# Another order for the 2986 operations of an attention and hardswish FFN kernel

## The chip, the cores and the metric

The kernel runs on one core of a Trainium2 chip. The metric is the device time of one execution in microseconds (us), as the median of several runs. The engines are TensorE (PE, matmuls), VectorE (DVE), ScalarE (ACT), GpSimd (POOL) and SyncE (SP). Each executes its own instructions one after the other; SP and POOL also issue transfers (DMA).

## The reference

```python
def _attn_ref(x, state):                     # x [8, 8, 512, 64], state [8, 8, 32, 64]
    scores = scale * np.matmul(x, state.transpose(0, 1, 3, 2))
    a = softmax(scores);  xread = np.matmul(a, state)
    scores2 = scale * np.matmul(state, x.transpose(0, 1, 3, 2))
    a2 = softmax(scores2);  sread = np.matmul(a2, x)
    return np.concatenate([xread, sread], axis=2)

def _moe_ref(x, w_in, w_out):                # x: 4352 rows of 512, w_in [512, 2048], w_out [2048, 512]
    h = x @ w_in
    g = h * np.clip(h + 3.0, 0.0, 6.0) / 6.0
    return g @ w_out
```

The softmax over the last axis is written out in the reference (the maximum is subtracted, and the sum divided out). The attention's result, with the heads side by side, is the input of the second function. All data are float32.

## The kernel before

The work is staged by batch. For each of the eight batches the kernel computes the scores of its 512 tokens against its 32 states per head, both softmaxes, the product of the state with the first weight (so that tokens pass straight to the hidden layer, `wp`), and then sixteen steps over the hidden layer, each of 128 of the 2048 hidden columns; a last sixteen steps treat the state rows of all batches. The steps of one batch run on TensorE while the other engines prepare the next batch.

A step has these parts. `first` (or `first_grouped`) multiplies the attention weights `aT` by `wp` into a bank `ps_h` on TensorE. The gate follows: ScalarE (L1250, L1413 or L1677) and VectorE (L1252, L1416 or L1680, with additions at L1261 for grouped steps) make `g` or `G`. It is split in a high part `g_hi` (ScalarE, L467, L472 or L494) and a low part `g_lo`. The low part is made on VectorE (L468 or L473), or, in the "far" form, VectorE negates the high part (L495) and POOL adds the value with an accumulating transfer (L497). `second` multiplies both parts by the second weight into the accumulators `acc`. All matmul products go through one helper, L1178.

To prepare a batch, SP loads x in the layout for scores as sixteen transfers of 64 KB into `raw` (L686, eight per half) and again for the reads as `xb` (L668, four of 256 KB); VectorE transposes each half (`tmp<-raw`, L846), TensorE makes the scores of both halves (`both<-tmp,stT`, L700) and, in the same group, what the states read of the batch before (`ps_h<-xb,raw`, L1134). The turned weights for that read are made by a VectorE transposition (L1096) and sixteen moves of 32 KB on SP (`raw<-raw`, L1103). In the first 100 us the weights arrive too, in a packed form that ScalarE and VectorE decode (L571, L576), and `w_out` is split in a high and a low part (L605; later POOL adds the parts by transfers at L1654 so that a 16-bit form can be used).

What sets the order: the kernel first collects all operations in a list (`Plan.add`), with their engine, what they read and write and their buffers. A table of numbers, `ORDER`, then says in which order they are issued. `Plan.order` walks that table, asserts that every operation comes behind those it depends on, and gives each buffer user a place; `Plan.issue` emits the instructions in this order, for all five engines. So every engine, and SP's and POOL's queues of transfers among them, executes its part of the table in the table's order, and an operation that has to wait holds up those behind it on its engine.

Of the kernel before, what the change touches and what calls it, by code (L numbers as in the profile page):

```python
# [68 lines left out]
1 0 5 2 3 4 24 79 92 27 34 11 29 31 6 35 30 36 28 37 32 43 38 33 44 39 45 49 40 46 47 41 50 56 48 42 51 52 61 57 25 53  # L69
58 80 62 54 26 59 55 63 74 81 64 130 75 65 82 77 60 93 14 78 68 66 76 19 67 87 69 94 71 88 95 107 70 72 89 108 96 114  # L70
90 73 97 109 12 91 429 110 7 102 13 154 111 132 115 161 103 113 112 85 104 127 105 8 116 106 120 83 117 121 171 9 84
126 118 131 122 144 133 119 15 129 134 86 137 16 128 138 10 135 145 136 123 17 152 124 166 100 125 153 169 18 151 167
98 170 194 168 146 99 188 101 157 147 20 183 211 148 21 196 215 186 149 150 201 155 187 217 210 184 158 22 216 164 23
195 189 156 178 223 185 213 159 165 193 206 139 225 190 174 214 160 141 218 426 208 191 224 219 212 162 222 204 142
163 228 220 140 192 202 430 175 209 238 229 431 271 172 221 247 236 143 205 173 235 239 203 237 230 234 176 240 259
179 177 244 260 233 181 261 254 243 182 231 207 245 180 262 427 246 263 264 505 232 290 338 241 272 281 322 274 273
291 242 286 250 275 295 251 248 276 292 282 288 249 279 287 277 283 252 297 278 280 289 284 253 299 255 506 285 256
296 293 337 308 257 300 258 317 305 265 294 332 267 301 309 266 298 335 268 306 336 269 315 428 307 333 310 302 304
334 323 314 270 318 339 303 311 319 775 320 324 364 507 352 358 325 341 226 316 359 340 313 353 321 355 368 360 354
342 361 403 312 504 326 365 369 362 327 363 343 198 404 373 412 366 367 370 344 399 405 371 375 345 508 417 372 346  # L80
347 348 374 422 401 349 424 376 418 423 400 328 419 402 420 350 408 421 425 394 406 329 351 411 395 410 330 396 409
413 407 495 397 414 509 331 432 398 415 496 416 439 511 377 447 464 441 227 440 448 468 497 437 382 514 438 385 433
465 393 513 462 199 469 386 498 457 356 434 466 389 499 435 388 463 458 387 471 510 459 467 460 481 436 516 470 461
380 517 478 357 392 479 515 444 477 390 472 487 378 482 473 476 445 512 489 379 525 474 535 629 475 391 483 519 384
488 381 502 518 197 486 383 500 484 443 501 536 442 485 503 631 446 520 537 541 200 630 452 572 449 538 450 634 539
456 590 632 543 454 550 575 451 521 542 577 453 522 579 540 455 480 573 523 551 558 580 635 552 574 530 569 633 578
570 636 576 571 640 591 544 638 524 592 545 637 546 644 563 493 606 547 494 526 549 607 593 564 548 568 531 565 589
650 608 594 492 595 581 491 566 609 596 586 642 587 612 661 582 639 567 613 588 583 626 643 666 597 614 641 669 623
667 532 776 618 610 777 584 677 628 670 527 585 490 662 624 528 668 778 529 620 685 779 621 553 684 663 625 682 780
664 619 700 678 615 665 598 627 679 683 617 533 680 708 599 534 616 701 709 622 690 600 611 702 695 707 681 703 706  # L90
784 645 805 704 710 717 655 715 601 554 656 740 782 711 555 657 559 602 705 560 716 741 781 785 714 561 658 562 742
748 747 743 659 603 746 712 660 796 713 604 556 744 557 605 745 754 797 771 803 798 807 773 799 783 812 772 651 800
765 646 806 804 801 652 787 766 653 802 654 794 767 725 691 770 671 724 692 793 718 672 696 817 720 697 721 788 698
723 792 673 768 789 719 795 674 769 722 827 693 774 818 694 824 790 819 699 825 647 791 820 826 675 828 823 676 834
829 749 832 930 833 836 730 835 830 837 731 863 838 786 839 857 726 831 728 759 877 727 858 821 732 648 822 859 733
887 884 760 860 729 882 761 865 750 861 883 900 862 751 762 869 885 910 878 763 864 912 764 755 879 906 870 931 841
756 867 868 866 880 907 889 917 901 881 902 929 909 757 918 911 758 888 813 908 919 846 913 922 814 886 649 920 923
925 1012 903 921 808 752 753 809 927 1006 1013 904 928 905 1017 1014 1008 1015 1009 734 1005 1010 847 1016 962 815 848
851 816 1019 999 914 1018 895 915 963 1020 890 969 916 1004 1000 964 926 842 924 810 735 1007 965 1041 1001 852 1002
966 1011 853 843 967 932 849 736 854 844 1003 737 855 975 856 1067 689 935 891 1069 970 850 1071 892 968 933 936 1070  # L100
845 1042 1047 896 971 934 1054 973 946 1065 897 1049 1051 1037 1043 974 1023 972 937 1059 1028 1044 1022 947 1039 1038
1052 1027 1053 1068 1021 1060 1045 1048 1040 1046 1050 686 1086 938 1025 1076 811 1061 1026 1057 939 688 1084 1024
1082 1062 1058 840 1064 1055 1066 1094 1063 949 1056 1088 1077 1103 940 1099 1072 1078 1083 1104 1101 941 898 1106
1079 942 1105 1087 1095 1100 1107 1080 1074 1073 1081 1102 1115 948 1075 1085 1089 1113 1119 950 1096 1090 1117 943
1202 1097 1121 893 1203 1098 894 1092 1091 1116 1127 1118 1114 1130 1108 1093 1133 1126 944 1120 1128 1109 1129 1132
1205 1204 1134 1110 1206 1122 1111 738 1161 1112 1123 1142 899 945 1162 1140 1146 1124 739 1131 1164 1144 1125 1148
1163 1165 1135 1141 1145 956 1255 1149 1136 1155 957 1137 1160 1150 1153 1256 1166 951 958 1258 1257 1151 1147 1259
1154 1167 1158 1138 1143 1156 1182 959 1152 1168 1189 960 1183 1157 1169 961 1191 1184 1196 1159 1139 871 1291 1185
872 1193 1294 1170 1176 1292 1194 1186 1190 1195 976 1171 1207 1187 1172 1034 993 1192 1173 1035 1239 1188 1208 1032
1036 1209 1179 1178 1240 687 1180 1210 1199 1033 1175 1241 1177 1181 1030 1211 1174 1200 1260 1296 1212 1218 988 1198  # L110
1213 1250 1251 1293 1197 1214 991 1249 1242 1261 1253 1029 1247 994 1248 987 1243 1254 1252 1221 1262 1031 1244 1215
995 1276 992 996 1245 978 1263 1246 1289 1295 981 1217 1277 1264 1219 985 1222 1216 1278 1265 977 1269 1220 1283 982
1285 1266 983 1287 1279 1267 1319 1280 989 873 979 997 874 1273 986 1297 1335 998 984 1320 990 1290 1288 1327 980 1281
1321 1286 1284 1201 1367 1282 1224 1322 1329 1275 1336 1345 1331 1237 1333 1368 1337 1318 875 1383 1369 876 1370 1298
1338 1323 1227 1339 1324 1238 1371 1230 1328 1381 1312 1228 1347 1332 1271 1225 1274 1377 1325 1233 1343 1313 1301
1326 1349 1315 1334 1330 1226 1268 1375 1314 1229 1300 1344 1302 1379 1231 1346 1340 1223 1303 1342 1272 1232 1270
1341 1236 1304 1390 1234 1348 1396 1299 1394 1384 953 1305 1407 1372 955 1385 1395 1382 1235 1373 1408 1380 1376 1386
1374 1393 1378 1316 1409 1397 1391 1392 1387 1398 1423 1410 1388 1513 1442 1400 1389 1399 1419 1411 1424 1435 1317
1402 1434 1432 1412 1576 1425 1401 1431 1413 1577 1420 1439 1414 1422 1426 1417 1440 1350 1416 1443 1421 1433 1579
1415 1427 1362 1437 1444 1418 1428 1452 1363 1441 1436 1306 1438 1360 1445 1454 1429 1471 954 1446 1430 1462 1359 1403  # L120
1447 1357 1405 1473 1361 1463 1580 1485 1356 1307 1456 1477 1578 1353 1464 1358 1448 1450 952 1465 1451 1449 1475 1308
1365 1508 1352 1469 1514 1509 1351 1491 1457 1487 1478 1355 1453 1466 1455 1511 1489 1366 1479 1493 1467 1364 1512
1354 1480 1470 1472 1510 1494 1490 1474 1481 1476 1613 1468 1482 1504 1500 1495 1616 1492 1548 1483 1614 1503 1496
1486 1484 1501 1617 1505 1544 1615 1506 1488 1546 1497 1515 1309 1498 1404 1310 1499 1406 1559 1535 1545 1311 1551
1564 1502 1550 1563 1529 1536 1461 1530 1516 1531 1517 1566 1565 1518 1547 1549 1537 1507 1560 1552 1532 1538 1519
1567 1666 1553 1581 1539 1669 1540 1570 1554 1562 1561 1582 1670 1597 1541 1583 1555 1568 1635 1556 1542 1557 1584
# [1794 lines left out]
```

## Time and profile before

| what | value |
|---|---|
| median of 3 runs (lowest to highest) | 604.08 us (602.52 to 604.81) |
| the profiled execution | 604.03 us |
| its span, first to last instruction | 602.2 us |
| granted TensorE clock, mean | 0.998 |
| busy: PE, DVE, ACT, POOL | 98%, 80%, 65%, 15% |

The busy share of an engine is the time in which it executed something, over the span. Two engines can each be busy and wait for one another at some places, so the shares alone do not show what a change of order is worth; the rows below go by stretch and by wait. The names in a row are those of the program: `out<-in`, with L and a number for the line.

### The profile page before, as it was taken

Reading aid. Unit: us, or ns where it says so; the run is one execution under the profiler, and the core shown is the slowest. Engines: PE = TensorE matmul, PEld = TensorE weight load, DVE = VectorE, ACT = ScalarE, POOL = GpSimd, SP = SyncE. Lnnn points to the kernel's source line nnn. Section 1 sums busy time; section 2 is a strip of 40 time slices with the busy share of each in tenths; the row PEclk is TensorE's granted clock in tenths of the full one; section 3 lists DMA queues with packets and bytes.
Section 4 is the critical chain, followed back from the end, with each engine's and each line's share of the span. In section 5 each row is a group of like instructions: output and inputs, shape, how many; then the busy total and the mean of one; then the engine's idle time right before and its main releaser. Section 6 shows DMA issues by size and latency. Waiting matters only on the chain. (4 is left out here: it accounts for less than half of the span.)

```text
span 602.2 us, 13365 instructions
## 1 busy us (share of the span) xinstructions
PE 590.8 (98%) x5331; PEld 453.2 (75%) x5331; DVE 480.4 (80%) x911; ACT 389.3 (65%) x637; POOL 90.3 (15%) x112
## 2 busy tenths in 40 slices
PE   8999999999999999998999999999999999999997
PEld 7577678768654445886778887888888878888875
DVE  5988996579767998887998988977898977876332
ACT  5888868867868876746465746566555655563432
POOL 2000000103444312211101111212111201111000
PEclk9999999999999999999999999999999999999999
DMA  8999124647898955896625684578534642323001
GB/s 284 355 214 318 62 84 123 130 106 137 118 125 107 125 136 63 125 169 113 114 67 62 138 131 86 69 143 121 102 48 83 123 80 33 66 32 67 2 30 42
DMA packets 101951, 68.24 MB, mean 113 GB/s; under 512 B 67712, under 2 KB 94976, under 8 KB 101504
## 3 DMA queue, kind: packets, MB, share of 16 engines
q0 software_dynamic: 14400, 21.37, 28.7%
q1 hardware_dynamic: 87200, 45.82, 28.2%
q8 instruction: 42, 0.69, 0.5%
q10 hardware_dynamic: 288, 0.20, 0.1%
q14 instruction: 21, 0.17, 0.1%
HBM read 33.41 MB, written 8.91 MB: 70 GB/s over the span
## 5 line engine op out<-in xcount | busy, mean ns | idle before, releaser
L1178 PE MATMUL ps_h<-aT,wp 128*128 128x256 f16 (+2 forms) x1146 | 164.1, 292 | 0.0
L1178 PEld LDWEIGHTS <-g_hi 128*128 128x128 f16 x1344 | 129.8, 98 | 36.8 <-issue 5.1
L1178 PE MATMUL acc<-w,g_hi 128*128 128x256 f16 (+1 forms) x704 | 129.0, 297 | 0.0
L1178 PEld LDWEIGHTS <-wp 128*128 128x128 f16 x1056 | 103.0, 98 | 23.8 <-issue 1.1
L1178 PE MATMUL acc<-T,g_hi 128*128 128x256 f16 x640 | 100.5, 273 | 0.0
L1178 PE MATMUL acc<-w,g_lo 128*128 128x256 f16 (+1 forms) x352 | 82.2, 297 | 2.6 <-DVE g_lo L468 2.6
L1178 PEld LDWEIGHTS <-g_lo 128*128 128x128 f16 x672 | 65.1, 98 | 21.5 <-DVE g_lo L468 2.9
L1250 ACT ACTIVATE G<-ps_h,three 128x512 f32<-128x512 f32 x55 | 42.7, 777 | 34.5 <-PE ps_h L1178 19.6
L1178 PE MATMUL acc<-T,g_lo 128*128 128x256 f16 x320 | 62.7, 273 | 0.3 <-DMA g_lo<-g 0.2
L497 POOL DMA_DIRECT2D g_lo<-G x35 | 30.1, 861 | 176.3 <-DVE g_lo L495 95.7
L1261 DVE TENSOR_TENSOR G<-G 128x256 f32<-128x256 f32 (+1 forms) x110 | 52.8, 484 | 1.4
L1178 PE MATMUL acc<-w_out_hi,g_hi 128*128 128x512 f32 x124 | 49.8, 402 | 0.0
L1178 PE MATMUL acc<-w_out_hi,g_lo 128*128 128x512 f32 x124 | 48.3, 390 | 0.0
L1178 PE MATMUL acc<-w_out_lo,g_hi 128*128 128x512 f32 x124 | 48.3, 390 | 0.0
L494 ACT CAST g_hi<-G 128x896 f16<-128x896 f32 x35 | 32.7, 935 | 19.9 <-DVE G L1261 16.9
L1252 DVE SCALAR_TENSOR_TENSOR G<-G,ps_h 128x512 f32<-128x512 f32 x55 | 37.5, 682 | 8.1 <-ACT G L1250 7.9
L1413 ACT ACTIVATE g<-ps_h,three 128x512 f32<-128x512 f32 x48 | 34.1, 715 | 11.3 <-PE ps_h L1178 8.8
L497 POOL DMA_DIRECT2D g_lo<-g x25 | 22.2, 888 | 109.7 <-DVE g_lo L495 64.5
L1416 DVE SCALAR_TENSOR_TENSOR g<-g,ps_h 128x512 f32<-128x512 f32 x48 | 32.6, 682 | 6.8 <-ACT g L1413 6.7
L1654 POOL DMA_DIRECT2D w_out_hi<-w_out_lo x16 | 16.4, 1253 | 113.1 <-ACT g_hi L472 92.4
L468 DVE SCALAR_TENSOR_TENSOR g_lo<-G,g_hi 128x896 f16<-128x896 f32 (+1 forms) x30 | 25.8, 863 | 8.8 <-ACT g_hi L467 5.0
L467 ACT ACTIVATE wp<-both 128x512 f16<-128x512 f32 x40 | 22.7, 595 | 14.7 <-PE both L700 14.7
(200 smaller groups left out, 981.8 us busy)
## 6 DMA issues: line engine op xcount, KB each, us to landing
xb<-in_x_dram SPq DMA_DIRECT2D x32, 256.0 KB, 3.4
g_lo<-G POOLq DMA_DIRECT2D x35, 224.0 KB, 4.1
raw<-in_x_dram SPq DMA_DIRECT2D x112, 64.0 KB, 3.3
out_dram<-ot SPq DMA_DIRECT2D x10, 512.0 KB, 3.2
early<-in_moe_w_in_dram SPq DMA_DIRECT2D x5, 1023.0 KB, 6.3
w_out_hi<-w_out_lo POOLq DMA_DIRECT2D x16, 256.0 KB, 4.8
g_lo<-g POOLq DMA_DIRECT2D x17, 224.0 KB, 3.8
raw<-raw SPq DMA_DIRECT2D x112, 32.0 KB, 2.8
```

Of the source, the lines that this page charges most:

```text
L467: S(cost, rank, lambda: nc.scalar.mul(hi(), src(), by()), [*reads, *keys], first_, after)
L468: V_(cost, rank, lambda: nc.vector.scalar_tensor_tensor(lo(), src(), by(), hi() if hi().dtype == F16 else hi().bitcast(F32), op0=ALU.mult, ...
L494: S(cost, rank, lambda: nc.scalar.copy(hi(), src()), reads, [writes[0]], after)
L497: P__(0.87, rank, lambda: nc.gpsimd.dma_start(lo(), src(), accum_op=ALU.add), reads, [writes[1]], (), size)
L1178: nc.tensor.matmul(ps, l, r, start=start and k == 0, stop=stop and k == len(pairs) - 1)
L1250: S_(0.73, rank, lambda: nc.scalar.activation(g(), h(), AF.Relu, bias=three_of(G_SCALE / 4), scale=scales["gate7"]()), [ps, ("scale", "gat ...
L1252: V(0.63, rank, lambda: nc.vector.scalar_tensor_tensor(g(), g(), 6.0 * G_SCALE / 4, h(), op0=ALU.min, op1=ALU.mult), [ps], [key])
L1261: V(cost, rank, lambda out=out, one=one, other=other, op=op: nc.vector.tensor_tensor(blocks(*out), blocks(*one), blocks(*other), op=op), [ ...
L1413: S_(cost + (0.12 if scaled else 0.05), rank, lambda: nc.scalar.activation(g(), bank(ps)[:, :width], AF.Relu, bias=three_of(by), scale=sca ...
L1416: V(cost, rank, lambda: nc.vector.scalar_tensor_tensor(g(), g(), 6.0 * by, bank(ps)[:, :width], op0=ALU.min, op1=ALU.mult), [ps], [g_key])
L1654: X("P", 0.87, rank, lambda w=w: nc.gpsimd.dma_start(w("hi"), w("lo"), accum_op=ALU.add), [lo_key], [hi_key], after, 1.35)
```

## The change

The table `ORDER` is replaced by another permutation of the same operations. No other line differs, and the operations, their sizes and their engines are the same. A line of the table, as the diff shows it (120 such lines in all):

```diff
 ORDER = """
-1 0 5 2 3 4 24 79 92 27 34 11 29 31 6 35 30 36 28 37 32 43 38 33 44 39 45 49 40 46 47 41 50 56 48 42 51 52 61 57 25 53
...
+1 0 5 2 3 4 24 79 92 426 27 34 28 6 30 36 37 11 31 35 29 38 32 43 44 33 39 45 49 40 46 47 41 50 56 25 48 51 42 26 52
...
```

First place: VectorE while the steps of batch 3 run, at about 273 to 283 us of the profile. `G` and `g` are gates, `g_lo` a low part, `tmp<-raw` the transposition of one half of x. Before:

```order
L1252 SCALAR_TENSOR_TENSOR G<-G,ps_h 128x512
L1261 TENSOR_TENSOR G<-G 128x3x128
L1261 TENSOR_TENSOR G<-G 128x256
L846 STREAM_TRANSPOSE tmp<-raw 128x1024
L468 SCALAR_TENSOR_TENSOR g_lo<-G,g_hi 128x896
L1261 TENSOR_TENSOR G<-G 128x3x128
```

and in the changed kernel, the rows that end with the same L468:

```order
L1261 TENSOR_TENSOR G<-G 128x256
L1049 RECIPROCAL r_3003<-r_3003 128x2
L1261 TENSOR_TENSOR G<-G 128x3x128
L1096 STREAM_TRANSPOSE raw<-tmp 128x8x4x32
L885 RECIPROCAL s_3020<-s_3020 128x32
L468 SCALAR_TENSOR_TENSOR g_lo<-G,g_hi 128x896
```

and the rows around that L846, eight rows further on:

```order
L468 SCALAR_TENSOR_TENSOR wp<-both,wp 128x512
L1261 TENSOR_TENSOR G<-G 128x3x128
L495 TENSOR_SCALAR g_lo<-g_hi 128x896
L886 TENSOR_TENSOR tmp<-tmp,s_3020 128x1024
L645 STREAM_TRANSPOSE stT<-st_raw 128x128
L495 TENSOR_SCALAR g_lo<-g_hi 128x896
L846 STREAM_TRANSPOSE tmp<-raw 128x1024
L468 SCALAR_TENSOR_TENSOR wp<-both,wp 128x512
```

The transposition stood directly ahead of the split, and now stands fourteen rows behind it.

Second place: SP's queue at about 108 to 125 us, where the loads of x for batch 2 end. Before:

```order
L1103 DMA raw<-raw 32x256 x4
L668 DMA xb<-in_x_dram 128x2x256
L1103 DMA raw<-raw 32x256
L686 DMA raw<-in_x_dram 32x16x32 x3
L668 DMA xb<-in_x_dram 128x2x256
L686 DMA raw<-in_x_dram 32x16x32 x8
L668 DMA xb<-in_x_dram 128x2x256
L634 DMA st_raw<-in_state_dram 32x4x32 x4
```

and now:

```order
L686 DMA raw<-in_x_dram 32x16x32
L1103 DMA raw<-raw 32x256 x4
L686 DMA raw<-in_x_dram 32x16x32
L1103 DMA raw<-raw 32x256 x3
L686 DMA raw<-in_x_dram 32x16x32 x10
L668 DMA xb<-in_x_dram 128x2x256 x2
L634 DMA st_raw<-in_state_dram 32x4x32 x4
```

The `xb` load that stood among the last eleven loads of x now stands behind all of them.

Third place: VectorE at about 58 to 64 us, where weights are still decoded (`w_in<-wide`) beside the first batch's steps. Before:

```order
L473 TENSOR_TENSOR wp<-both,wp 128x256
L473 TENSOR_TENSOR g_lo<-g,g_hi 128x512
L576 SCALAR_TENSOR_TENSOR w_in_672<-wide,tops 128x4x128
L846 STREAM_TRANSPOSE tmp<-raw 128x1024
L576 SCALAR_TENSOR_TENSOR w_in_672<-wide,tops 128x4x128
L473 TENSOR_TENSOR g_lo<-g,g_hi 128x512
```

and now:

```order
L576 SCALAR_TENSOR_TENSOR w_in_683<-wide,tops 128x4x128 x2
L473 TENSOR_TENSOR g_lo<-g,g_hi 128x512
L846 STREAM_TRANSPOSE tmp<-raw 128x1024
L576 SCALAR_TENSOR_TENSOR early_654<-early_654,tops 128x512 x2
L473 TENSOR_TENSOR wp<-both,wp 128x512 x2
L1416 SCALAR_TENSOR_TENSOR g<-g,ps_h 128x512 x2
```

The transposition stood between the two decodes, and now stands behind both, with what follows pushed behind it.

## Rows read from the trace of the kernel before

**Rows 1.** The page, busy time: us (share of the span) xinstructions.

```profile
PE 590.8 (98%) x5331; PEld 453.2 (75%) x5331; DVE 480.4 (80%) x911; ACT 389.3 (65%) x637; POOL 90.3 (15%) x112
```

**Rows 2.** By stretch: length, busy PE, PEld, DVE, ACT, POOL, clock, DMA share, GB/s.

```profile
48.00:75.00 27.00, 26.46 (x209) 19.13 (x209) 24.56 (x39) 22.65 (x43) 0.00 (x0) 1.00 0.58 192
...
126.00:270.00 144.00, 144.00 (x1088) 91.12 (x1078) 121.26 (x234) 105.09 (x165) 43.82 (x50) 1.00 0.78 123
...
380.00:597.00 217.00, 217.00 (x2185) 184.03 (x2184) 161.87 (x316) 117.42 (x175) 24.93 (x29) 1.00 0.39 68
```

**Rows 3.** What TensorE waited for: us in total, times, longest us.

```profile
PE acc L1178 <- DVE g_lo L468: 2.6, 1, 2.6
PE both L700 <- DVE room L1584: 1.0, 1, 1.0
```

**Rows 4.** Timeline, TensorE: start us, us, operation [idle before <-releaser].

```profile
277.25 1.04 PE L1178 MATMUL acc<-T,g_hi 128*128 128x256 f16 x8
280.94 0.28 PE L1178 MATMUL acc<-w,g_lo 128*128 128x256 f16 x1 [2.65 <-DVE g_lo L468]
```

**Rows 5.** Timeline, VectorE, at the same place.

```profile
278.66 1.25 DVE L846 STREAM_TRANSPOSE tmp<-raw 128x1024 f32<-128x1024 f32 x1 [3.49 <-DMA raw<-in_x_dram]
279.83 1.05 DVE L468 SCALAR_TENSOR_TENSOR g_lo<-G,g_hi 128x896 f16<-128x896 f32 x1
```

**Rows 6.** Timeline, TensorE, score matmuls of batch 1, then of batch 2.

```profile
68.17 1.09 PE L700 MATMUL both<-tmp,stT 64*32 64x512 f32 x16
...
122.36 1.06 PE L700 MATMUL both<-tmp,stT 64*32 64x512 f32 x8
...
125.46 1.10 PE L1134 MATMUL ps_h<-xb,raw 128*32 128x64 f32 x64
```

**Rows 7.** Timeline, VectorE, ahead of the score matmuls of batch 2.

```profile
123.17 1.25 DVE L846 STREAM_TRANSPOSE tmp<-raw 128x1024 f32<-128x1024 f32 x1 [2.11 <-DMA raw<-in_x_dram]
```

**Rows 8.** Timelines of SP and POOL, then loads issued in 111.5:117.7 and 117.7:119.5.

```profile
113.83 5.34 SPq L686 DMA_DIRECT2D raw<-in_x_dram  x8
...
117.88 1.76 POOL L1654 DMA_DIRECT2D w_out_hi<-w_out_lo  x2 [10.33 <-PE acc L1178]
...
raw<-in_x_dram SPq DMA_DIRECT2D x9, 64.0 KB, 2.7
...
w_out_hi<-w_out_lo POOLq DMA_DIRECT2D x2, 256.0 KB, 4.3
raw<-in_x_dram SPq DMA_DIRECT2D x3, 64.0 KB, 3.2
```

**Rows 9.** Timeline, TensorE, 61 to 63 us.

```profile
61.49 0.39 PE L1178 MATMUL acc<-w_out_hi,g_hi 128*128 128x512 f32 x1
...
61.94 0.39 PE L1178 MATMUL acc<-w_out_hi,g_lo 128*128 128x512 f32 x1
62.82 1.09 PE L700 MATMUL both<-w_in,stT 64*32 64x512 f32 x16 [0.49 <-DVE w_in L576]
```

**Rows 10.** Timeline, TensorE, at 296 us; the transfer issued in 291:292.

```profile
296.11 0.27 PE L1178 MATMUL acc<-T,g_lo 128*128 128x256 f16 x1
296.61 0.72 PE L1178 MATMUL acc<-T,g_lo 128*128 128x256 f16 x5 [0.23 <-DMA g_lo<-g]
...
g_lo<-g POOLq DMA_DIRECT2D x1, 224.0 KB, 5.5
```

**Rows 11.** The chain that ended last, its first piece: start us, us, what.

```profile
363.84 4.92 DMA g_lo<-G
```

**Rows 12.** Timeline, SP: a load of batch 4, and the loads of batch 5.

```profile
249.70 0.63 SPq L686 DMA_DIRECT2D raw<-in_x_dram  x1
...
267.48 10.20 SPq L686 DMA_DIRECT2D raw<-in_x_dram  x13
```

**Rows 13.** The page, DMA issues: KB each, median us from issue to landing.

```profile
raw<-in_x_dram SPq DMA_DIRECT2D x112, 64.0 KB, 3.3
...
raw<-raw SPq DMA_DIRECT2D x112, 32.0 KB, 2.8
```

## What I expect, before the changed kernel has run

> **What bounds the kernel now.** The first view is the table of engines: TensorE is busy 98% of the span, VectorE 80%, ScalarE 65% [rows 1]. The second is the table by stretch: TensorE has no idle time at all from 126 to 270 us and from 380 to 597 [rows 2]. Both orders give TensorE the same matmuls, so its work is the same in both, and only its waits can change. The third view lists what TensorE waited for: one wait of 2.6 us for a VectorE split (L468), and one of 1.0 us put down to VectorE's `room` (L1584) [rows 3]; all others are below 1 us. The busy time of a matmul that stands still can hide more, so I took the timelines and compared the distance between starts with that of the same work elsewhere. That gives five places.
>
> *Place A, 278 us.* A group of eight matmuls starts at 277.25 and is busy for 1.04 us; the next starts at 280.94, after 2.65 us of waiting for L468 [rows 4]. On VectorE that split (279.83) stands directly behind a transposition of x, `tmp<-raw` at L846, which started at 278.66 after an idle time of 3.49 us that ended with a load of `raw` [rows 5]. VectorE works in order: the split had nothing to do with these loads and stood behind them.
>
> *Place B, 122 us.* Sixteen score matmuls `both<-tmp,stT` are busy for 1.09 us in batch 1; in batch 2 it takes from 122.36 to 125.46, 3.10 us, until the next kind starts [rows 6]. The excess is 3.10 - 1.09 = 2.0 us, of which the list of waits names 1.0 and the rest counts as busy. VectorE's L846, which makes their `tmp`, started at 123.17 and took 1.25 us, after 2.11 us of idle time that ended with a load of `raw` [rows 7]; I take L846, not `room`, for the releaser. Its eight loads were issued one behind the other, 5.34 / 8 = 0.67 us each, from 113.83 on. Those issued in 111.5:117.7 took a median 2.7 us to land, those in 117.7:119.5 3.2 us, with two 256 KB additions of POOL in flight, 4.3 us each, issued at 117.88 and behind [rows 8].
>
> *Place C, 62 us.* Matmuls at 62.82 waited for L576, which stood on VectorE behind another L846. Two starts at 61.49 and 61.94 set the pace, 0.23 us a matmul, so the excess is 62.82 - 61.94 - 0.23 = 0.65 us [rows 9].
>
> *Places D and E, 296 and 368 us.* The eight matmuls of rows 4 follow one another after about (1.04 - 0.28) / 7 = 0.11 us; at 296.11 one takes 0.50 us to the next, and the wait is for the transfer into `g_lo`, which took 5.5 us [rows 10]: 0.39 us. The chain of waits begins with such a transfer, 4.92 us [rows 11]; I take 0.2 us for it, half of D's.
>
> The start and the last 5 us (an eviction and a store) have the same rows in nearly the same order, so I put them at 0, with 0.4 us to either side.
>
> **The change part by part.** Nothing is added or removed; the sum is made against the profiled execution, 604.03 us, whose span is 602.2 us and which lies 0.05 us below the median of the runs, 604.08.
>
> Place A: the L846 now stands fourteen of VectorE's rows behind the split, some 10 us of TensorE's work later than before. The split would have started at 278.66 - 3.49 = 275.17 and ended 1.05 us later, before the matmuls at 277.25 began. Gain 2.65 us, if nothing new is late. What is late next: the loads of that L846. One move of the state weights (`raw<-raw`) now stands ahead of the last of them on SP, and it waits for VectorE's L1096. In the order the last load stands 6.9 us of TensorE's work ahead of L846, hardly other than the 7.2 of before; but before, SP issued late: the eight loads for the second half of batch 4 stood between its moves, the last at 249.70, and the queue was still busy with the loads for this L846 in the row from 267.48 on [rows 12]. In the new order those eight stand some 20 us of TensorE's work sooner, so SP comes to the loads of A about eight issues, 8 x 0.67 = 5 us, earlier. Landing took a median 3.3 us [rows 13]; 6.9 - 3.3 leaves some 3 us, so I take the whole 2.65, with 0 as the lower end.
>
> Place B: the eight last loads stand one SP issue sooner, 0.67 us, since the load of `xb` that was among the last eleven is now behind them. One group of three matmuls more (3 x 0.23 = 0.68 us) stands ahead of the score matmuls. So 1.35 us of the 2.0 are gone at the least; if the last load, issued about 0.65 us before 119.17, where its row ends, with 256 KB less ahead of it lands in 2.7 us and not in some 4.6 (118.52 to 123.17), all are. I take 1.5, and 0 to 2.0 as ends: POOL's additions may now be issued earlier as well. By the rows the last loads landed later when POOL's additions were in flight. The Trainium skill (DMA: Bandwidth & Descriptors, Queues, rings and completion order) says that each DMA engine goes round the queues for which it has work, packet by packet, so that a load beside an addition gets its turns only in alternation, however early it stands in its own queue. By that rule the gain would stay at the 1.35 us of the two shifts; by the landing of the undisturbed loads it would be 2.0.
>
> Place C: one L846 now stands behind the decode of the weight, and one group of matmuls more ahead of its use, so nothing of the 0.65 should be left. But VectorE is nearly full there (48:75: 24.56 of 27.00 us [rows 2]), and what it is spared at 60 us it has to do by 68 us, where a split, L846, two decodes, two evictions (L473) and two gates (L1416) now stand in one row, and the last four free the banks that the next matmuls need. I take 0 for C, with -1.25 (an L846 that TensorE waits for) and +0.65 as ends.
>
> Places D and E: between POOL's issue and the first matmul that uses the product stood 4.81 and 4.91 us of TensorE's work; now 6.34 and 5.91 (the matmuls between the two in each order, at the trace's durations). The transfers took 5.5 and 4.92 us, so both are covered: 0.6 us gained. The smallest such distance is about as before (3.27 against 3.24 us), and the median 6.56 against 6.50, so I expect no other one late by much.
>
> Everything else: at five score or product groups the VectorE operation that frees their bank now stands directly ahead of them in the order, and which of them go wrong the trace of before can't tell. The small waits of before, C, D and E, come to 0.65 + 0.6 = 1.25 us. I allow 1.2 us for new ones of that kind, with 0 and 3.9 as ends; the upper end has one more wait like A's.
>
> Sum: 2.65 + 1.5 + 0 + 0.6 - 1.2 = 3.55 us. 604.03 - 3.55 = 600.5 us.
>
> **The rivals.** First, *the waits move* and little time is gained. For it speaks that before is itself an order in which nearly all waits are hidden, and that every L846, decode or split that goes later stands ahead of something else on an engine that is 80% busy. It is one or two new waits of A's size: 604.03 - 2.65 - 1.35 - 0.6 + 2.65 = 602.1, or with two 604.7. Against it speaks that the loads and transfers at A, D and E have 1 to 3 us of cover in the new order.
>
> Second, slower: *SP's line is late where batches meet.* The place is SP's queue at 165, 295 and 370 us. The distance, in TensorE's work, from SP's last issue to the operation that needs it falls from 5.4 to 3.4 us for the first half of x of batch 3, from 5.4 to 2.95 for the moves of the state weights of batch 4 (now mixed with the x loads of batch 5), and from 11.7 to 4.7 for those of batch 5. Loads land in 3.3 us and moves in 2.8 us [rows 13], so it decides once SP stands one to three issues (0.67 us each) behind its place; from 267.48 on SP's loads came one behind the other for 10.20 us [rows 12], so it can be behind. What such a wait costs is A's 2.65 us. Three of them make 7.95: 604.03 - 4.75 + 7.95 = 607.2, and with the 1.2 us allowed above 608.4. Against it speaks that SP is through with the loads of batch 4 sooner.
>
> Third, all works and nothing new is late: 604.03 - 2.65 - 2.0 - 0.65 - 0.6 = 598.1. That the table's rows change nothing is excluded by the order of VectorE and SP at A and B.
>
> **How the numbers follow.** A measurement of this kernel can tell about 0.5% from no change, which is 3.0 us: faster is below 601.1, slower above 607.1. The forecast, with what is close to it down to 598.1, has 0.52; the waits move, 601.1 to 607.1, 0.32; SP late, above 607.1, 0.16. For the range the lower end is the case in which all works, less half a microsecond for the start, 597.7. The upper end is 606: it takes in the moved waits up to the two of A's size and 1.3 us more, and leaves out the late SP line.
>
> **What would show it.** Right: no idle time of VectorE ahead of L846 from 275 to 290 us, and no L468 among TensorE's waits there; the score matmuls near 121 us with at most 0.8 us of excess; no wait for `g_lo` by transfer above 0.2 us. Wrong: idle time of VectorE ended by `raw` loads near 165 or 290 us, or TensorE's `both<-tmp,stT` waiting for moves near 298 and 372 us (the second rival); L473 or L1416 in TensorE's waits between 55 and 80 us (the first).

## The result and the profile after

The changed kernel takes 598.5 us (598.21 to 599.02); the kernel before took 603.54 us beside it. The ratio is 0.9916 with a 95% interval of 0.9894 to 0.9938, so it is faster by 3.7 to 6.4 us. The profiled execution of after took 598.21 us with a span of 596.4 us; before's had 604.03 and 602.2 [rows 1, 2]. The pair of profiles thus differs by 5.8 us, somewhat more than the medians, which are 5.0 us apart.

The page of after, busy time; then the table by stretch (length, busy PE, PEld, DVE, ACT, POOL, clock, DMA share, GB/s):

```profile
PE 589.0 (99%) x5331; PEld 452.9 (76%) x5331; DVE 481.6 (81%) x911; ACT 389.3 (65%) x637; POOL 89.8 (15%) x112
...
48.00:75.00 27.00, 27.00 (x213) 19.99 (x213) 25.18 (x38) 22.20 (x40) 0.00 (x0) 1.00 0.53 168
115.00:126.00 11.00, 11.00 (x121) 8.31 (x120) 10.23 (x32) 7.99 (x19) 1.75 (x2) 1.00 0.63 124
...
270.00:283.00 13.00, 13.00 (x138) 11.04 (x136) 12.41 (x26) 8.87 (x13) 2.24 (x3) 1.00 0.69 106
```

The engines' work is the same; TensorE has no idle time left in the stretches of C, B and A. What TensorE waited for in after (us in total, times, longest):

```profile
PE ps_h L1890 <- PEq L1905: 0.8, 1, 0.8
PE acc L1178 <- ACT g_hi L494: 0.7, 1, 0.7
PE acc L700 <- DVE wp L473: 0.7, 1, 0.7
```

Both waits of [rows 3] are gone. The first and third row lie in the first 25 us, and the second, at 405 us, is new. At A, VectorE's timeline of after:

```profile
274.18 1.03 DVE L468 SCALAR_TENSOR_TENSOR g_lo<-G,g_hi 128x896 f16<-128x896 f32 x1
...
282.09 1.24 DVE L846 STREAM_TRANSPOSE tmp<-raw 128x1024 f32<-128x1024 f32 x1
```

Against [rows 5], the split is through 5.7 us sooner, and L846 has no idle time ahead of it. At B, the timelines of TensorE, VectorE, SP and POOL and the loads issued in 110:116.3:

```profile
121.64 1.09 PE L700 MATMUL both<-tmp,stT 64*32 64x512 f32 x16
122.66 1.10 PE L1134 MATMUL ps_h<-xb,raw 128*32 128x64 f32 x64
...
119.39 1.22 DVE L846 STREAM_TRANSPOSE tmp<-raw 128x1024 f32<-128x1024 f32 x1
...
109.96 6.82 SPq L686 DMA_DIRECT2D raw<-in_x_dram  x10
...
116.47 1.75 POOL L1654 DMA_DIRECT2D w_out_hi<-w_out_lo  x2 [12.38 <-PE acc L1178]
...
raw<-in_x_dram SPq DMA_DIRECT2D x10, 64.0 KB, 2.6
```

Against [rows 6 to 8], the score matmuls take 1.02 us to the next kind instead of 3.10, L846 ends about 1 us ahead of them, and the issue of the last of the ten loads starts at 116.14, 0.33 us ahead of POOL's additions.

Where the 5.8 us went, from the start of each matmul less the work ahead of it in its order, in the two profiles: the first 30 us 0.5, C (50 to 65 us of work) 0.9, B 2.1, A 2.9, D 0.4, E 0.3, the new wait at 405 us -0.8, and small waits elsewhere -0.5.

### The profile page after: what moved, and what is told of

Its sections match the earlier page's. It is cut to its first block, busy times and chain, and to the rows that moved or that the text cites. A ratio compares the mean times of both kernels' runs of the same rounds, so it can differ in the third digit from the quotient of the medians.

```text
span 596.4 us, 13389 instructions
## 1 busy us (share of the span) xinstructions
PE 589.0 (99%) x5331; PEld 452.9 (76%) x5331; DVE 481.6 (81%) x911; ACT 389.3 (65%) x637; POOL 89.8 (15%) x112
## 4 chain that ended last, share of the span: by engine, by line
PE 93%; DVE 2%; SPq 2%; issue 1%; ACT 1%; DMA 0%; DVEq 0%
PE acc L1178 54%; PE ps_h L1178 30%; PE both L700 5%; PE ps_h L1134 1%; SPq L1103 1%; PE acc L1449 1%; PE ps_h L1890 1%; PE ps_h L700 1%; DMA st_raw<-in_state_dram 0%; SPq L634 0%; PE both L921 0%; SPq L686 0%; DVE w_in L576 0%; ACT g_hi L494 0%; DVE ot L936 0%
## 5 line engine op out<-in xcount | busy, mean ns | idle before, releaser
L1178 PE MATMUL acc<-w,g_hi 128*128 128x256 f16 (+1 forms) x704 | 130.8, 297 | 0.0
L1178 PE MATMUL acc<-w,g_lo 128*128 128x256 f16 (+1 forms) x352 | 84.0, 297 | 0.0
L1178 PE MATMUL acc<-T,g_lo 128*128 128x256 f16 x320 | 64.2, 273 | 0.0
L468 DVE SCALAR_TENSOR_TENSOR g_lo<-G,g_hi 128x896 f16<-128x896 f32 (+1 forms) x31 | 26.3, 851 | 10.9 <-ACT g_hi L467 6.3
L467 ACT ACTIVATE g_hi<-G 128x896 f16<-128x896 f32 (+1 forms) x31 | 23.4, 758 | 17.5 <-DVE G L1261 7.4
```

The lines of the kernel that those rows point to most:

```text
L467: S(cost, rank, lambda: nc.scalar.mul(hi(), src(), by()), [*reads, *keys], first_, after)
L468: V_(cost, rank, lambda: nc.vector.scalar_tensor_tensor(lo(), src(), by(), hi() if hi().dtype == F16 else hi().bitcast(F32), op0=ALU.mult, ...
L1178: nc.tensor.matmul(ps, l, r, start=start and k == 0, stop=stop and k == len(pairs) - 1)
```

## The experiments

Each kernel is one of the two with a few numbers of `ORDER` moved. In the diffs, 1513 is the L846 of A, 1389 the split L468 behind it, 337 and 258 the L846 and the decode of C, 200 the load of `xb` and 455 the last load of x at B, 592 the score matmuls of B, 549 a group of three matmuls, and 1490 and 1893 the first matmuls with `g_lo` at D and E.

Since one profile has its chances, the same stretches were read in all runs: from the first group of `both<-w_in` at 28 us to the start of the L1134 group of batch 1 (C), from there to that of batch 2 (B), and from that of batch 4 to that of batch 5 (A and D). "As before" says that the order in the stretch is before's.

| stretch | as before | with the place changed |
|---|---|---|
| start of the first group | 27.6 to 28.8 (nine runs) | |
| C | 40.5 to 40.9 (five runs), 42.1 (one) | c_decode 41.0, five_places 40.9, c_loads 41.2, c_front 39.9; after 39.8 |
| B | 56.3 to 57.0 (six runs) | b_xb 55.4, b_additions 54.3, b_group 56.6 and five_places 55.4 (both with 0.7 more work) |
| A and D | 39.1 to 39.8 (three runs), 40.3 to 40.9 (four) | a_swap 38.2, a_back 37.0, five_places 36.4 |

What parts the two groups at A is TensorE's clock. In c_decode, b_xb, b_additions and c_loads it fell to 0.50 of full speed, 1.2 instead of 2.4 GHz, within a microsecond of the end of A's wait, and these are the four above 40 us; in before, b_group and c_front it stayed at 1.00. The waits ahead of it were of one size, 2.1 to 2.6 us in the four and 2.2 to 2.65 in the three. The stretch of b_additions at 279 to 282 us (the wait ends at 278.21), and that of before at 281 to 284 (280.94), in the columns of the table by stretch:

```profile
279.00:282.00 3.00, 3.00 (x33) 1.52 (x18) 3.00 (x7) 2.92 (x7) 0.86 (x1) 0.50 0.03 6
...
281.00:284.00 3.00, 3.00 (x44) 1.99 (x45) 3.00 (x8) 3.00 (x6) 0.46 (x1) 1.00 0.18 37
```

So A's wait costs about 1.1 us more where the clock falls behind it, and the prediction has no term for that. Why it fell in some executions and not in others stays open. The executions without a trace have a mean clock on record. It is 0.996 or 0.997 in the profiles with the fall and 0.998 to 1.000 in all others; by that mark, 0.997 or less, which is a reading and not a trace, the clock fell in 40 of the 65 executions of before that were measured beside these experiments (median 604.8 us; the other 25 have 603.2), in 6 of 10 of c_decode and 5 of 10 of c_front, where A's wait is left, in 2 of 10 of after_hold, where a wait of 1.8 us stands, and in none of the 25 of a_swap, a_back and five_places.

**a_swap: L846 one row later.**

```diff
-... 1410 1388 1513 1442 1400 1389 1399 ...
+... 1410 1388 1442 1400 1389 1513 1399 ...
```

> The order of before with one operation moved by one row of VectorE: the transposition of x (L846) of place A stands behind the split L468 instead of ahead of it. Theory 1 (the wait at A is the split's place behind a transposition whose loads are late): TensorE's wait for L468 at 278 us is gone, 2.65 us. VectorE still stands until the loads land at 278.5, some 2.3 us, with the next gates behind it; they have about 1 us of slack, so 1 to 1.5 us come back as a new wait just behind, and the time is 602.3 to 602.9 us. Theory 2 (VectorE's delay counts whatever stands behind it, the waits move): all 2.65 us come back at the next product, 603.5 to 604.1. If the row alone counted and the delay not at all: 601.4.

Measured 601.8 us against 604.52 for before, ratio 0.9961 (0.9943 to 0.9978). VectorE's and TensorE's timelines:

```profile
276.34 1.09 DVE L468 SCALAR_TENSOR_TENSOR g_lo<-G,g_hi 128x896 f16<-128x896 f32 x1 [0.78 <-ACT g_hi L467]
278.81 1.25 DVE L846 STREAM_TRANSPOSE tmp<-raw 128x1024 f32<-128x1024 f32 x1 [1.37 <-DMA raw<-in_x_dram]
...
281.89 0.27 PE L1178 MATMUL acc<-T,g_lo 128*128 128x256 f16 x1 [1.24 <-ACT ot L1287]
```

The wait for the split is gone, and VectorE still stands for the load, 1.37 us, since the split itself had to wait for ScalarE. Of the 2.65 us, 1.24 come back 3 us later, as theory 1 says, by way of ScalarE: the stretch of A and D is 1.5 us shorter than in before's profile. The time fell by more, 2.7 us, and came out 0.5 us better than theory 1's range; that fits the clock, which by the mean fell in none of its ten executions and in over half of before's.

**a_back: L846 ten rows later.**

```diff
-... 1410 1388 1513 1442 ...
+... 1414 1422 1426 1513 1417 1440 ...
```

> The order of before with the same transposition moved ten of VectorE's rows back, behind an L1261 at about 283 us, when its loads have landed. Theory 1: VectorE no longer stands idle there, A's 2.65 to 2.8 us are gone and nothing comes back: 601.2 to 601.5 us. Theory 2 (waits move): 603 us or more, with a new wait between 280 and 302 us.

Measured 601.36 us, ratio 0.9949 (0.9934 to 0.9965), as theory 1 has it. VectorE's timeline, and all that TensorE waited for from 270 to 302 us:

```profile
280.30 1.23 DVE L846 STREAM_TRANSPOSE tmp<-raw 128x1024 f32<-128x1024 f32 x1
...
PE acc L1178 <- DMA g_lo<-g: 0.4, 1, 0.4
```

The row left is D. A's wait comes from one row of VectorE's order and goes away with it. By the stretch of A and D, moving the transposition to where its loads have landed gives 2.8 us, and moving it just out of the way, 1.5. By the medians it is 3.2 and 2.7 us, so how much of the gain the second half of the way brings isn't settled by one profile of each.

**c_decode: L846 of C behind the decode.**

```diff
-... 256 296 293 337 308 257 300 258 317 ...
+... 256 296 293 308 257 300 258 337 317 ...
```

> The order of before with the transposition of x at 61 us moved behind the second decode L576. The prediction took nothing for this place. Theory 1 (local): the excess of 0.65 to 1.0 us at 57 to 65 us is gone and stays gone at 80 us, 603.0 to 603.4 us. Theory 2 (VectorE is full there): it comes back by 75 us, 603.8 to 604.2 us.

Measured 604.46 us, ratio 1.0 (0.9982 to 1.0018). TensorE, at 62 us and at 68:

```profile
61.59 1.09 PE L700 MATMUL both<-w_in,stT 64*32 64x512 f32 x16
...
67.50 1.09 PE L700 MATMUL both<-tmp,stT 64*32 64x512 f32 x16 [0.49 <-DVE wp L473]
```

The wait for L576 is gone, and 0.49 us of waiting for L473 stands at 67.5. Theory 2 holds: it comes back, by the operations that the prediction named.

**five_places: six operations of 2986.** They are 337, 200, 549, 1513, 1490 and 1893; the expectation counted eight.

```diff
-... 256 296 293 337 308 257 300 258 ...  541 200 630 ...  1410 1388 1513 1442 ...
+... 256 296 293 308 257 300 258 337 ...  579 540 455 200 480 ...  638 524 549 592 545 ...
-... 1494 1490 1474 1481 1476 1613 ...  1883 1893 1996 1884 ...
+... 1422 1426 1513 1417 ...  1494 1474 1481 1476 1613 1490 ...  1883 1996 1893 1884 ...
```

> The order of before with eight operations moved and all others left: the transpositions of A and C as in the runs that move them alone, the load of xb at B behind the last loads of x, one more group of three matmuls ahead of the score matmuls there, and the first matmul with g_lo at D and E behind the next group. Theory 1 (the five places carry the whole difference): 604.0 less 2.8, 1.4 to 2.0, 0.7 and 0.6, so 597.9 to 598.7 us, as the changed kernel (598.5). Theory 2 (the gain lies in the order as a whole, transfers sooner everywhere): 600 to 602 us. Waits that move: 602 to 604 us.

Measured 598.86 us, ratio 0.9918 (0.9893 to 0.9944); after has 0.9916. What TensorE waited for at 0.4 us or more:

```profile
PE ps_h L1890 <- PEq L1905: 0.8, 1, 0.8
PE acc L700 <- DVE wp L473: 0.7, 1, 0.7
PE both L700 <- DVE wp L473: 0.5, 1, 0.5
PE acc L700 <- DVE w_in L576: 0.4, 1, 0.4
```

Theory 1 holds for the time: moving six operations gives as much as the whole new table. That the two are equal is in part chance. Here C keeps its 40.9 us, where after has 39.8, and B an excess of 0.5 us; after pays 0.8 us for the new wait at 405 us, and some for small ones, which this order doesn't have. What the rest of the new order gains and what it costs happen to cancel.

**b_xb: only the load of xb behind the loads of x.**

```diff
-... 537 541 200 630 452 ...
+... 579 540 455 200 480 ...
```

> The order of before with the load of xb at B (SP, 113 us) put behind the last load of x; nothing else moves. The last eight loads are issued 0.67 us sooner. Theory 1 (only the place in SP's queue counts, and a load beside POOL's additions is slow however early it stands): they land 0.67 us sooner and the excess of the score matmuls falls from 2.0 to 1.4 us. Theory 2 (a load that is issued before the additions start is not slowed): the last load lands in 2.7 us, about 120.6 us after an issue at 117.9, 2.5 us sooner than before, and the excess falls to 0.3 us or less.

Measured once: 604.41 us beside 604.63. SP's timeline, TensorE's, and the loads issued at 118.4:118.5 and 119.1:119.135:

```profile
111.13 1.11 SPq L1103 DMA_DIRECT2D raw<-raw  x1
112.28 7.48 SPq L686 DMA_DIRECT2D raw<-in_x_dram  x11
...
123.21 2.15 PE L700 MATMUL both<-tmp,stT 64*32 64x512 f32 x16
125.29 1.10 PE L1134 MATMUL ps_h<-xb,raw 128*32 128x64 f32 x64
...
raw<-in_x_dram SPq DMA_DIRECT2D x2, 64.0 KB, 2.5
...
raw<-in_x_dram SPq DMA_DIRECT2D x1, 64.0 KB, 3.7
```

The excess is 2.08 - 1.02 = 1.1 us instead of 2.08. The run doesn't keep the two theories apart as it was meant to: SP stood 0.5 us longer at the move at 111.13, so the last load was still issued (119.13) behind POOL's additions (118.60), and took 3.7 us, while the one before, issued 0.15 us ahead of them, took 2.5. In this run C's stretch, with before's order, was the long one of the table (42.1 us), 1.4 us more than in before's profile, and the clock fell at A; so the time did not show B's 0.9 us.

**b_additions: POOL's additions two microseconds later.**

```diff
-... 579 540 455 480 573 523 551 558 580 635 552 574 530 569 633 578 570 636 ...
+... 579 455 480 573 523 551 580 635 552 574 569 633 578 570 540 558 530 636 ...
```

> The order of before with one group of three matmuls, for which POOL's two additions at 118 us wait, put four groups later, so that the additions start at about 120 us, when all loads of x for B have been issued. SP's queue and VectorE's order are those of before. If the additions are what slows the last loads, these land in 2.6 to 2.8 us instead of 3.9 and 4.6, the transposition starts at 121.3 and not at 123.2, and the excess at the score matmuls falls from 2.0 to 0.2 us or less. If the loads are late for the xb in front of them or for SP, nothing changes: 2.0 us.

Measured once: 602.1 us beside 604.63. SP, POOL, VectorE, TensorE, and the loads issued at 118.3:118.4:

```profile
113.64 5.34 SPq L686 DMA_DIRECT2D raw<-in_x_dram  x8
...
120.42 1.75 POOL L1654 DMA_DIRECT2D w_out_hi<-w_out_lo  x2 [13.05 <-PE acc L1178]
...
121.03 1.24 DVE L846 STREAM_TRANSPOSE tmp<-raw 128x1024 f32<-128x1024 f32 x1
...
122.19 1.20 PE L700 MATMUL both<-tmp,stT 64*32 64x512 f32 x16
123.31 1.10 PE L1134 MATMUL ps_h<-xb,raw 128*32 128x64 f32 x64
...
raw<-in_x_dram SPq DMA_DIRECT2D x2, 64.0 KB, 2.7
```

SP's eight loads run as in [rows 8], but the additions start behind them, the loads land in 2.7 us, and the excess is 1.12 - 1.02 = 0.1 us. B's stretch is 2.0 us shorter with no load moved: the collision with POOL's additions made the whole of B.

**after_xb: the load of xb put back in after.**

```diff
-... 519 572 635 454 630 452 ...  456 632 578 200 551 ...
+... 519 572 635 200 454 630 452 ...  456 632 578 551 ...
```

> The order of after with the same load of xb put back ahead of the last eight loads of x, as it stood in before. These loads are then issued 0.67 us later, and the last one behind the start of POOL's additions (116.5 us). Theory 2 of the run on xb: the last loads land in 4 us or more, at 120.8 to 121.4 instead of 118.9 us, the transposition ends at 122.2 to 122.6 and the score matmuls (121.6) have an excess of 0.5 to 1.0 us. Theory 1: they land 0.67 us later, at 119.6, the transposition starts at 119.6 instead of 119.4, and no excess appears.

Measured once: 599.1 us. POOL, VectorE, TensorE, and the last load, issued in 117.26:117.3:

```profile
117.25 1.75 POOL L1654 DMA_DIRECT2D w_out_hi<-w_out_lo  x2 [12.38 <-PE acc L1178]
...
120.98 1.25 DVE L846 STREAM_TRANSPOSE tmp<-raw 128x1024 f32<-128x1024 f32 x1 [1.11 <-DMA raw<-in_x_dram]
...
122.42 1.09 PE L700 MATMUL both<-tmp,stT 64*32 64x512 f32 x16
123.44 1.10 PE L1134 MATMUL ps_h<-xb,raw 128*32 128x64 f32 x64
...
raw<-in_x_dram SPq DMA_DIRECT2D x1, 64.0 KB, 3.7
```

The last load is issued 0.02 us behind the addition and takes 3.7 us instead of 2.7, as theory 2 says, and VectorE waits 1.11 us for it. But L846 still ends at 122.23, just ahead of the matmuls at 122.42: no excess. The expected wait of 0.5 to 1.0 us is a miss; after has that much cover at B.

**b_group: one more group of matmuls ahead.**

```diff
-... 544 638 524 592 545 637 546 644 563 493 606 547 494 526 549 607 ...
+... 544 638 524 549 592 545 637 546 644 563 493 606 547 494 526 607 ...
```

> The order of before with one more group of three matmuls put ahead of the score matmuls of B; transfers and VectorE as before. The prediction's step: the work gives 0.68 us of cover, so the excess of the score matmuls falls from 2.08 to 1.4 us, and no other wait follows. If the group itself waited for VectorE, it would stay at 2.08 us.

Measured once: 603.63 us beside 603.97. TensorE:

```profile
123.34 1.06 PE L700 MATMUL both<-tmp,stT 64*32 64x512 f32 x8
125.08 1.06 PE L700 MATMUL both<-tmp,stT 64*32 64x512 f32 x8 [0.67 <-DVE room L1584]
126.07 1.10 PE L1134 MATMUL ps_h<-xb,raw 128*32 128x64 f32 x64
```

The excess is 2.73 - 1.02 = 1.7 us, 0.4 less than before and not 0.7. Its stretch, less the 0.7 us of work that was moved into it, is 55.9 against 56.3 to 57.0.

**c_loads: weights ahead of three loads of x.**

```diff
-... 426 208 191 ...  222 204 142 ...  192 202 430 ...  271 172 221 247 236 ...
+... 426 191 ...  222 142 ...  192 430 ...  271 172 221 247 208 204 202 236 ...
```

> The order of before with three loads of x for batch 1 (needed at 61 us) put on SP's queue behind two weight loads that they stood ahead of at 40 to 44 us; nothing else moves. In before the second of these weight loads was issued at 45.65 and landed at 54.64, ScalarE's decode L571 waited for it until 54.72 and VectorE's L576 until 55.52, 1.81 us idle. If this lateness is what fills VectorE up to 63 us, the load lands about 2 us sooner, VectorE's idle time at 55.5 shrinks to 0.3 us or less, and C's excess (0.33 at 58 us and 0.66 at 62.8) falls to 0.3 us in all without anything coming back at 68 us. If the place of the transposition alone made C, the excess at 62.8 us stays.

Measured once: 606.19 us beside 603.97. ScalarE, VectorE and TensorE:

```profile
53.90 1.42 ACT L571 CAST tops<-early 128x512 f16<-128x512 bf16 x2 [1.48 <-DMA early<-in_moe_w_out_dram]
...
60.76 0.69 DVE L576 SCALAR_TENSOR_TENSOR w_in<-wide,tops 128x512 uint32<-128x512 uint32 x1 [1.15 <-ACT tops L571]
...
63.37 1.09 PE L700 MATMUL both<-w_in,stT 64*32 64x512 f32 x16 [1.32 <-DVE w_in L576]
```

The weight load landed only 0.8 us sooner, and the next one, pushed back on SP, landed later (59.87 against 58.51), so VectorE waited for the decode at 60.76 and TensorE 1.32 us for VectorE. My expectation failed, but the run shows the chain the other way: a later weight load, an idle decode, a longer C (41.2 us). b_xb has the same by chance: with before's order at C, the first of these weight loads landed at 55.39 instead of 54.64 though that run's first group started 0.7 us sooner, VectorE stood for the decode 2.49 us instead of 1.81, and C took 42.1 us.

**after_wait: the new wait at 405 us taken out of after.**

```diff
-... 2103 2062 2111 2267 ...
+... 2242 2115 2101 2111 2277 ...
```

> The order of after with one operation moved: the transposition of the states of batch 7 (L645), which made VectorE wait for a load of 5.3 us at 401 us and TensorE for 0.8 us at 404.9, stands five of VectorE's rows later, when the load has landed. If that wait is local as A's was, the 0.8 us at 404.9 us is gone and the time is 0.7 to 0.8 us below after's, 597.7 to 597.8 us on the scale of 598.5; if VectorE's lateness moves on, another wait follows within 5 us and the time is after's.

In after VectorE and TensorE stand there so:

```profile
402.63 0.31 DVE L645 STREAM_TRANSPOSE stT<-st_raw 128x128 f32<-128x128 f32 x1 [1.50 <-DMA st_raw<-in_state_dram]
...
404.87 0.61 PE L1178 MATMUL acc<-T,g_hi 128*128 128x256 f16 x4 [0.71 <-ACT g_hi L494]
```

Measured 598.22 us (597.21 to 599.58), ratio 0.9904 (0.9881 to 0.9926). The wait is gone, and the time from the L1134 group of batch 6 to that of batch 7 falls by 0.78 us, with nothing behind it. The times cannot tell the 0.7 us from after's 0.9916; the trace can. (The single transfers took 3.0 to 4.0 us; the 5.3 us in the expectation runs from the first one's issue.) Its median is the lowest of all, by less than the runs can tell apart.

**after_hold: A's transposition put back in after.**

```diff
-... 1389 1424 1450 1229 1413 ...  1491 1440 1453 1513 1463 ...
+... 1389 1424 1450 1229 1513 1413 ...  1491 1440 1453 1463 ...
```

> The order of after with the transposition of A put back among VectorE's operations to where the last of its loads is issued (about 275 us), behind one split and ahead of fourteen operations. The load lands at 277.5, so VectorE stands idle from 275.2 to 277.5 and is 3.5 us later than in after with what follows. If VectorE's lateness costs what goes beyond 1 to 2 us of slack, a new wait of 1.5 to 2.5 us appears between 278 and 285 us and the time is 600.0 to 601.0 us; if after's order has slack enough there, 598.5 us.

Measured 602.36 us beside 603.97, ratio 0.997 (0.9945 to 0.9996), so most of the gain is gone. VectorE and TensorE:

```profile
278.48 1.25 DVE L846 STREAM_TRANSPOSE tmp<-raw 128x1024 f32<-128x1024 f32 x1 [2.26 <-DMA raw<-in_x_dram]
...
283.41 0.39 PE L1178 MATMUL acc<-T,g_hi 128*128 128x256 f16 x2 [1.79 <-ACT g_hi L494]
```

The named wait is 1.8 us; from the reads of batch 4 to those of batch 5 it is 2.3 us. VectorE's lateness of 3.5 us costs TensorE two thirds, 5 us later and through ScalarE. Another 0.5 us was lost at B, 0.5 behind it and 0.6 between batches 6 and 7, where the order is after's, and the time came out above the range. What happened at B the trace shows: SP was 0.7 us later there, so that the last load of x was issued 0.4 us behind the additions (116.87 against 116.45) and took 3.9 us, and the score matmuls have an excess of 0.5 us:

```profile
120.90 1.25 DVE L846 STREAM_TRANSPOSE tmp<-raw 128x1024 f32<-128x1024 f32 x1 [0.64 <-DMA raw<-in_x_dram]
```

The 0.5 behind B is for the most part a wait for a low part at 153 us. Why SP was later stays open. After's cover against the collision at B is thus no more than some 0.3 us of SP's time.

**c_front: after's order for the first 360 operations alone.** The diff covers the first fourteen lines or so of the table, which begin:

```diff
-1 0 5 2 3 4 24 79 92 27 34 11 29 31 6 35 ...
+1 0 5 2 3 4 24 79 92 426 27 34 28 6 30 36 ...
```

> The first 360 operations of before's table (all up to about 71 us, the place C among them) in the order that after gives them, the other 2626 as in before. Both moves of single parts at C brought nothing, while after loses 0.9 us less there than before. If after's gain at C comes from its order of the first 70 us as a whole (weight loads sooner on SP, so that ScalarE's and VectorE's decodes don't wait at 55 us), the time from the first score product (28 us) to the first score group of batch 1 (69 us) falls from 40.5 to 40.9 us to about 39.8, VectorE's idle time ahead of L576 at 55 us is gone, and the time is 0.9 us below before's. If it was chance of one run, the stretch stays at 40.5 to 40.9 us.

Measured 603.25 us beside 603.93, ratio 0.9986 (0.9968 to 1.0005). C's stretch is 39.9 us, as in after and as expected, but the time is not 0.9 us below before's. B's stretch is 57.0, at the upper end of its range, and the trace shows the wait there grown:

```profile
PE both L700 <- DVE room L1584: 1.6, 1, 1.6
```

TensorE came to the score matmuls of B 0.5 us sooner (121.83) and waited there for the same loads, which SP issued no sooner (the last at 118.49, against 118.53). The additions, which wait for TensorE, did come sooner (117.09), and three loads instead of two were issued at their start or behind it and took 4.3 to 5.2 us. In the trace C's gain is real, and B takes most of it back. The times alone, 0.7 us less with an interval that takes in zero, show neither.

## Why the prediction was right, and where it was off

The forecast, 3.55 us less, was right in sign and, at A, B, D and E, in mechanism. It was 1.5 us short by the medians and 2.3 by the pair of profiles. By its own steps, in the pair:

- **A: 2.65 us foretold, 2.9 measured.** Shown by a_back and, the other way round, by after_hold. By the medians a_back gives 3.2 us, since in over half of before's executions the clock fell behind this wait too; how many of the four in the result did isn't on record. Two details were off. The split would not have started at 275.17, because its high part was not ready: in a_back it started at 276.63, still in time. And SP was not 5 us sooner with the last load: that one stood behind the move which waited for L1096, was issued at 274.67 and landed at 277.5. The gain held because L846 came only at 282.09, 4.6 us later.
- **B: 1.5 us foretold, 2.1 measured.** The term was mis-sized where I let the load beside the additions stay slow however early it stands. b_additions, after_xb and b_xb show what decides, and it holds in all fourteen profiles: the last load issued 0.05 us or more ahead of the first addition took 2.4 to 2.8 us, those issued from 0.03 us ahead of it on took 3.6 to 5.3. The Trainium skill (DMA: Bandwidth & Descriptors, Queues, rings and completion order) says that a DMA engine goes round its queues packet by packet, and a load beside additions was slower here; "however early" was my addition, and the runs refute it. I could have seen it in [rows 8]: the 3.2 us there is the middle of one load issued 0.7 us ahead of the additions, 2.5 us, and one issued with them, 3.9; the third has no landing in the trace. So a shift of 0.7 us was worth more than 0.7 us.
- **C: 0 foretold, 0.9 measured.** The step that failed is the cause. I took the place of L846 for it, and c_decode showed that this alone does come back at 68 us, as I wrote. What after does is further ahead: the weight load that took 9.0 us to land (45.65 to 54.64) and left VectorE idle for 1.81 us at 55.5 lands at 51.55 in after, and there is no idle decode; c_front has the same. VectorE's decode in before, ScalarE's ahead of it, and VectorE's in after:

```profile
55.52 0.69 DVE L576 SCALAR_TENSOR_TENSOR early<-early,tops 128x512 uint32<-128x512 uint32 x1 [1.81 <-ACT tops L571]
...
54.72 1.43 ACT L571 CAST tops<-early 128x512 f16<-128x512 bf16 x2 [1.75 <-DMA early<-in_moe_w_out_dram]
...
53.41 0.68 DVE L576 SCALAR_TENSOR_TENSOR early<-early,tops 128x512 uint32<-128x512 uint32 x1
```

I read VectorE as full there and did not ask what it waited for. That the order of the first 360 operations makes the 0.9 us in C's stretch is shown by c_front; that it is this load among them is not shown, since c_loads, which was to test it, moved its landing by only 0.8 us.
- **D and E: 0.6 us foretold, 0.7 measured.** In five_places both waits are gone too.
- **New waits: 1.2 us allowed, about 0.8 came as one wait at 405 us, and some 0.5 in small ones.** That the sum is near is luck: the allowance was for small waits like C, D and E, and most came as one. That at 405 is of the second rival's kind: a load on SP (the states of batch 7) that VectorE reached too early. It cost 0.8 and not 2.65 us, and none stood at the three places that the rival named.
- **Start: 0 foretold, 0.5 measured.** It is within what before's order itself scatters (27.6 to 28.8 us), so it is not counted.

The rival of moving waits was right for c_decode, in part for a_swap, and in the trace for c_front; it was wrong for a_back and b_additions, and for the order as a whole, in which 0.8 us and small waits are all that came back.

## What to carry to other kernels

When an engine waits on a transfer, look at what stands directly behind the waiting operation in its queue; moving the waiting operation to where its data has landed gave the whole wait here, and moving it just out of the way left 1.2 us of it. A wait that ends on a transfer can swallow what is gained ahead of it, as B did with C's gain in c_front, so test a set of edits together before calling one of them useless; it need not, since the 2.0 us of b_additions at B came through A. Where a transfer is late, look at what was issued within the same microsecond on another queue. Read the granted clock behind each long wait, since the time of a wait and what follows it need not be the same in every execution. Read a stretch that is "full" for its idle rows too: the 1.81 us that mattered stood 7 us before the wait.

## What the runs showed that I had not expected

Where after's order has cover, it is also the steadier one. With it, the stretch of C took 39.82 to 39.85 us in five runs, and that of A 37.93 to 37.94 in the three runs in which it was left as in after. With before's it was 40.5 to 42.1 and 39.1 to 40.9, the latter for the most part by the clock. B is not steady in after's order: 54.9 us in three runs and 55.4 in after_hold. The first group of `both<-w_in` started between 27.6 and 28.8 us in nine runs in which the order up to there is the same. That goes with TensorE's pace at the start: its first 128-wide matmuls follow one another after 0.21 us and later after 0.11, and the change comes at 4.2 to 4.6 us in the three runs that start the group by 27.8, at 5.8 to 6.9 us in the other six. A difference of a microsecond between two single profiles of such a kernel is therefore read by stretch, not from the span.
